# A list scheduler that counts all DMA queues as one resource, and constant matmuls that go on longer, in a sparse attention with two MLPs

## The chip, the cores and the metric

The kernel runs on one core of a Trainium2 chip. The metric is the device time of one launch in microseconds. The five engines are called TensorE (PE, with its weight loads PEld), VectorE (DVE), ScalarE (ACT), GpSimd (POOL) and SyncE (SP). SP only issues transfers; ScalarE and GpSimd issue some too, each on a queue of its own.

## The reference

Four batches, eight heads, 576 positions, head size 64. Four heads see the last 32 positions, four see every 32nd. The result (2304 tokens x 512) goes through two MLPs of width 2048, the first with a squared ReLU and an affine step, the second with a quadratic spline.

```python
def reference(**kw):
    attn_out = _attn_ref(q, k, v)                       # softmax(mask(scale * q k^T)) v
    x = attn_out.transpose(0, 2, 1, 3).reshape(B * S, H * D)
    x = _moe_ref(x, w_in, w_out, s, b)                  # (s * relu(x @ w_in)**2 + b) @ w_out
    return _moe2_ref(x, w_in2, w_out2)                  # h<=-1: 0, h>=1: h, else (h+1)**2/4; then @ w_out2
```

## The kernel before

The weights come as 64-bit words and are decoded on the chip: a piece (128 x 512, 512 KB as 64-bit words) is loaded into one of three `raw` buffers (`decode`, L337), ScalarE makes a float of its upper half (L348), VectorE shifts and joins it (L350, L352). Every operand of an MLP product is split in two (`hi`, `lo`), and each product is three matmuls: hi x hi, hi x lo, lo x hi (`mm3`, L707, and `mm3s`, L949). `weights` (L356) makes the split pieces `w0h`, `w0l` (first matrix) and `w1h`, `w1l` (second matrix) of the first MLP.

The tokens are cut into six units of 384. Attention goes over 21 tiles (`attend`, L439): a strided tile takes some residues of one batch, a local tile 256 tokens. For each tile TensorE writes the mask and the scores (`scores`, L569), VectorE and ScalarE make the softmax (L602 to L627), TensorE transposes it (`flip`, L633), ScalarE or VectorE copies that to SBUF as `pt` (L639), and TensorE forms the values product (`values`, L644), which is split into the MLP's operands `xh` and `xl` (L686 to L692). Half of the first MLP's hidden width is done by plain products (`hidden`, `output`); for the other half the second matrix, and in the second MLP both matrices, use Strassen's scheme with seven products (`product`, `hidden2`, `output2`). For this scheme sums of weight quarters are made on the chip, stored to DRAM through two `pp` buffers by GpSimd's queue (`prepare`, L372, and `parts`, L385; the store is L393), and loaded back by SP when needed (`wmat`, L865).

The order of the work is not written out. Each step is an `Op` with its engines and costs, put into an `Issue` (L109). `order()` (L161) is a list scheduler: backwards from the end it gives each step a due time (with a random offset of 0.3 us from the seed `SEED`), and then, forwards, it always takes the step that can start first, the earlier due time first among equals. Each engine issues its steps in the order of the planned starts; on the chip they wait for semaphores only. The planned times are therefore not those of the chip, but set the order on every engine and queue. MLP products are chained to one another (`pe_op`, L716, and `pe_block`, L946), so that attention products can only be placed between them.

The costs are functions: `dma` (L320) gives a load SP for its bytes at `DMA_RATE`, 390 GB/s, plus 0.08 us for each transfer, and 2.0 us until it has landed. Transfers on ScalarE's queue take 0.45 us of ScalarE each (`load`, L456), the stores (`STORE`, L370) 1.0 us of GpSimd and 4.0 us more to land, and the loads of pieces to prepare get 3.0 us extra (`RAW_LAG`).

While nothing else is ready for TensorE at the start, it multiplies a constant tile: ten times before all (L1180), and in `busy` (L564) before the scores of tiles 1 to 4 and before each tile's transposes, up to three products, if the planned start is before `FILL` = 24 us and as the planned idle time suggests.

Of the kernel before, what the change touches and what calls it, by code (L numbers as in the profile page):

```python
# [13 lines left out]
I64 = mybir.dt.int64  # L14
# [23 lines left out]
SW = 4 * 128 + 2 * RT * NJ + 4 * D  # L38
NEG = -8.0e9
AHEAD = 3.0  # L40
SEED, JITTER = 3, 0.3
WARM = 10
HI_ACT, HOLD, NACC = 12, (0, 1, 3), 6
FILL, MOST = 24.0, 3
RAW, DT, KB, QV, SM, PT, PP, TB = 3, 2, 4, 3, 3, 2, 2, 3
BUFS = {"kb": KB, "qv": QV - 1, "qx": 1, "sm": SM - 1, "sx": 1, "pt": PT}

# [17 lines left out]
G_TAGS = ["w1h", "w1l"] * 4 + ["w1hx", "w1lx"] * 4 + ["kb"] * 4 + ["pi"] * 4 + ["qx", "sx"] + ["qv"] * 2 + ["sm"] * 2 + ["pt"] * 2  # L65
S_TAGS = ["kb"] * 4 + ["qx", "sx"]
SPLIT, SUMMED, SUM_BACK, EVAC2 = (0.0, 6.0, 6.0), (0.0, 0.0, 0.0), 0, 5.0
RAW_LAG, STORE_LAG = 3.0, 4.0
COUNTED = 2
SPACE_A, SPACE_W = 5.2, 2.4  # L70


SUB, MUL, ADD = ALU.subtract, ALU.mult, ALU.add
LATENCY = 0.12
DMA_RATE = 390.0e3
DMA_LATENCY = 2.0
DMA_ISSUE = 0.45
BY_SLOT, ACC_ACT = 3, 0.38


# [28 lines left out]
class Issue:  # L109
# [51 lines left out]
    def order(self):  # L161
# [13 lines left out]
        rng = np.random.default_rng(SEED)  # L175
        for o in self.ops:
            o.due += JITTER * rng.standard_normal() - o.sooner
        free = {"port": 0.0}
        for o in self.ops:
            o.wait, o.ready = len(o.deps), 0.0  # L180
            for x in o.engs:
# [17 lines left out]
        while pool:  # L199
            best = None  # L200
            for o in pool:
                t = room(o)
                if t is None:
                    continue
                for e, d, _, *port in o.engs:
                    at = max(free[e], o.ready, t, free["port"] if port else 0.0)
                    key = (at + (d - min(x[1] for x in o.engs)), o.due, o.n, d, at)
                    if best is None or key < best[0]:
                        best = (key, o, e, d)
            if best is None:  # L210
                raise RuntimeError("the buffers don't suffice")
            (*_, at), o, e, d = best
            _, _, lag, *port = next(x for x in o.engs if x[0] == e)
            pool.remove(o)
            o.start, o.eng, o.idle = at, e, at - free[e]
            free[e] = at + d
            if port:
                free["port"] = at + d
            end = at + d + lag
            for b in o.allocs:  # L220
                b.ring.taken.append(b)
            for b in o.bufs:
                b.left -= 1
                b.end = max(b.end, end + LATENCY)
                b.near = max(b.near, at + d if e == "pe" else end + LATENCY)
            for q in o.succ:
                q.wait -= 1
                q.ready = max(q.ready, at if o in q.behind else at + d if q.engs[0][0] == e == "pe" else end + LATENCY)
                if not q.wait:
                    pool.append(q)  # L230
            done.append(o)
# [11 lines left out]
def sparse_attention_two_mlps(ctx: ExitStack, tc: tile.TileContext, loc, strd, w_ins, w_outs, fixed, out):  # L243
# [27 lines left out]
    op = plan.op  # L271
# [45 lines left out]
    def pool(n):  # L317
        return ("pool", 0.13 + n * 0.00224, 0.1, "port")

    def dma(n, count=1):  # L320
        return ("sp", max(n / DMA_RATE + 0.08 * count, DMA_ISSUE * count), DMA_LATENCY)

    def pe(t):
        return ("pe", t, 0.1)
# [10 lines left out]
    decodes, prepared, pi_line, w_loads, w0_line, w1_line, p_line = [], [], [], [], [], [], []  # L335

    def decode(src, after=(), allocs=(), t=None, line=None, raw=None):  # L337
        late = RAW_LAG if raw else 0.0
        raw = raw or buf(sp, "raw", [128, 2 * DM], I32, RAW)
        t = t or buf(sp, "dt", [128, DM], I32, DT)  # L340
        words = lambda i: raw.tile.rearrange("p (a b) -> p a b", b=2)[:, :, i]
        x = lambda: t.tile.bitcast(F32)
        q_, d_, lag_ = dma(src.shape[0] * src.shape[1] * 8)
        load = op(lambda e: e.dma_start(out=raw.tile.bitcast(I64), in_=src), [(q_, d_, lag_ + late)],
                  writes=[raw], after=after, allocs=allocs, line=line)


        first = op(lambda e: e.activation(out=x(), in_=words(1).bitcast(F32), func=AF.Prelu, scale=2.0 ** -112, alpha=-2.0 ** 32),  # L348
                   [act(DM)], [raw], [t])
        op(lambda e: e.tensor_scalar(out=t.tile, in0=t.tile, scalar1=3, scalar2=None, op0=ALU.logical_shift_left),  # L350
           [dve2(DM, 0.0005)], (), [t])
        op(lambda e: e.scalar_tensor_tensor(out=t.tile, in0=words(0), scalar=29, in1=t.tile,  # L352
                                            op0=ALU.logical_shift_right, op1=ALU.bitwise_or), [dve2(DM)], [raw], [t])
        return t, x, first, load
# [12 lines left out]
        decodes.append(first)  # L367
        wt[g, o] = (hi, lo)

    STORE = lambda nq: ("pool", 1.0, STORE_LAG)  # L370

    def prepare(o, i, early=False):  # L372

# [65 lines left out]
    def attend(i, early):  # L439
# [14 lines left out]
            return buf(wp if tag[0] == "w" else sp, tag, [128, 512], F32, BUFS.get(tag, MS // 2))  # L454

        def load(y, parts, size, queue="sp", line=a_line):  # L456
            ways = [dma(size, len(parts)) if queue == "sp" else ("act", DMA_ISSUE * len(parts), DMA_LATENCY + 2 * size / DMA_RATE)]
            first = bool(w_loads) and not held and line is a_line
            o = op(lambda e, i=i: [e.dma_start(out=f(), in_=x) for f, x in parts], ways, part=[y], line=line,
                   after=[w_loads[k] for k in HOLD] if first else ())  # L460
# [102 lines left out]

        def busy(e, first, out):  # L564

            for _ in range(min(int(first.idle / 0.25 + 0.6), MOST) if first.start < FILL else 0):
                e.matmul(out=out, lhsT=warm_t[:, 0:out.shape[0]], rhs=warm_t[:, 0:out.shape[1]], start=True, stop=True)

        def scores(e, i=i):  # L569
# [72 lines left out]
        pv = [buf(ps, "side", [128, 2, nv], F32, 2) for _ in range(2)]  # L642

        def values(e, i=i):  # L644
            if strided:
                for hp, g in ((hp, g) for g in range(2) for hp in range(2)):
                    for j, _, n, _, _, at_ in (x for x in groups2 if x[1] == g):
# [12 lines left out]
                                e.matmul(out=pv[blk].tile[half(par), hp, c:c + 32], lhsT=v4(pos)[half(blk), s, 2 * hp + par, :],  # L660
                                         rhs=pt.tile[half(blk), 2 * par + pos, r:r + 32], start=True, stop=True)

        op(values, [pe(0.62 if strided else 1.07)], [*vals, pt], pv)

        off, end, cs = (b * S, b * S + S, (2, 3)) if strided else (256 * d, 256 * (d + 1), (0, 1))
        for bank in range(2):
# [611 lines left out]
```

## Time and profile before

| | us |
|---|---|
| median of 3 runs | 839.2 (837.93 to 839.42) |
| the profiled execution | 835.43 |
| its span, first to last instruction | 833.6 |
| TensorE busy | 809.8 (97%) |
| VectorE, ScalarE, GpSimd busy | 627.3, 526.5, 92.3 |
| DMA read and written | 264 GB/s over the span |

Busy time says which engine has work, not which one makes others wait; that is in the chain of work that ended last, followed back from the end, and in the waits. The granted clock is a share of 2.4 GHz; it has two levels here, 0.5 and 1. A mean between them is a stretch with both.

### The profile page before, as it was taken

To read this page: it belongs to the slowest core of one execution; us is meant where nothing else is said; L and a number is where in the kernel's file an instruction comes from. 1 tells how busy PE (TensorE), PEld (TensorE's weight loads), DVE (VectorE), ACT (ScalarE), POOL (GpSimd) and SP (SyncE) were. 2 spreads that over 40 slices of the span, in tenths; PEclk is the share of its full clock that TensorE was granted. 3 is DMA by queue.
4 is the path that set the end of the run, shared out by engine and by line. 5 is a ranking of instruction groups with operands and counts; after the bars stand their busy time and mean duration, and the time that the engine had idled before them with its cause. 6 is when DMAs were issued, how large, how long until landed. Compare 5 with 4: busy or idle time off the path is not lost.

```text
span 833.6 us, 17675 instructions
## 1 busy us (share of the span) xinstructions
PE 809.8 (97%) x6263; PEld 788.5 (95%) x6263; DVE 627.3 (75%) x1335; ACT 526.5 (63%) x1120; POOL 92.3 (11%) x186
## 2 busy tenths in 40 slices
PE   6799999989999999999999999999999999999998
PEld 4679999979899999999998999999999999999998
DVE  4698539879665856768789989997477988466966
ACT  5586545564556666758576677965487854667653
POOL 2110012322212112121111010000000000000000
PEclk9599999999999999999999999999999999999999
DMA  8977484798666759889889899978988889888882
GB/s 260 275 222 253 136 261 159 263 307 276 240 228 246 243 200 335 291 301 337 287 291 314 264 396 386 312 249 270 305 251 256 253 252 293 287 248 253 251 268 94
DMA packets 107261, 221.15 MB, mean 265 GB/s; under 512 B 14118, under 2 KB 29606, under 8 KB 107174
## 3 DMA queue, kind: packets, MB, share of 16 engines
q1 hardware_dynamic: 95906, 182.89, 68.2%
q0 software_dynamic: 10240, 36.71, 11.6%
q8 instruction: 50, 0.82, 0.4%
q10 hardware_dynamic: 1028, 0.43, 0.2%
q14 instruction: 37, 0.30, 0.1%
HBM read 172.27 MB, written 47.71 MB: 264 GB/s over the span
## 4 chain that ended last, share of the span: by engine, by line
PE 89%; DMA 6%; DVE 2%; issue 1%; ACT 1%; SPq 0%; POOL 0%; ACTq 0%; POOLq 0%
PE acc L954 8%; PE acc L953 8%; PE acc L952 8%; PE h L709 8%; PE h L710 7%; PE h L711 7%; PE side L952 6%; PE side L953 6%; PE side L954 6%; PE acc L709 4%; PE h L954 3%; PE h L953 3%; PE h L952 3%; PE acc L710 3%; PE acc L711 3%; DMA kb<-in_strd 2%
## 5 line engine op out<-in xcount | busy, mean ns | idle before, releaser
L393 POOL DMA_DIRECT2D dw<-pp x80 | 55.1, 690 | 273.2 <-DVE pp L391 198.6
L709 PE MATMUL h<-xh,w0h 128*128 128x384 f32 x192 | 66.0, 344 | 0.0
L711 PE MATMUL h<-xh,w0l 128*128 128x384 f32 x192 | 64.8, 337 | 0.7 <-DVE w0l L364 0.7
L709 PE MATMUL h<-xh,w0hx 128*128 128x384 f32 x192 | 65.1, 339 | 0.0
L710 PE MATMUL h<-xl,w0h 128*128 128x384 f32 x192 | 64.8, 338 | 0.0
L711 PE MATMUL h<-xh,w0lx 128*128 128x384 f32 x192 | 64.4, 335 | 0.0
L710 PE MATMUL h<-xl,w0hx 128*128 128x384 f32 x192 | 64.4, 335 | 0.0
L736 ACT ACTIVATE t<-h 128x384 f32<-128x384 f32 x51 | 24.8, 487 | 45.5 <-PE h L711 45.2
L711 PEld LDWEIGHTS h<-xh,w0l 128*128 128x128 f32 x192 | 36.3, 189 | 1.0 <-DVE w0l L364 1.0
L709 PEld LDWEIGHTS h<-xh,w0h 128*128 128x128 f32 x192 | 36.4, 190 | 0.5
L710 PEld LDWEIGHTS h<-xl,w0h 128*128 128x128 f32 x192 | 36.3, 189 | 0.3 <-DVE xl L692 0.3
L709 PEld LDWEIGHTS h<-xh,w0hx 128*128 128x128 f32 x192 | 36.0, 188 | 0.3
L710 PEld LDWEIGHTS h<-xl,w0hx 128*128 128x128 f32 x192 | 36.1, 188 | 0.0
L711 PEld LDWEIGHTS h<-xh,w0lx 128*128 128x128 f32 x192 | 36.0, 188 | 0.0
L328 ACT ACTIVATE gh<-w1h 128x384 fp32r<-128x384 f32 x48 | 24.6, 522 | 14.6 <-PE acc L954 6.3
L999 DVE TENSOR_TENSOR gl<-w1h,gh 128x384 fp32r<-128x384 f32 x48 | 26.4, 555 | 9.6 <-ACT gh L328 9.4
L348 ACT ACTIVATE dt<-raw 128x512 f32<-128x512 f32 x42 | 27.7, 667 | 9.2 <-DMA raw<-in_w_ins 6.8
L709 PE MATMUL acc<-gh,w1hx 128*128 128x384 f32 (+1 forms) x96 | 33.4, 348 | 0.0
L709 PE MATMUL acc<-gh,w1h 128*128 128x384 f32 (+1 forms) x96 | 33.2, 346 | 0.0
L711 PE MATMUL acc<-gh,w1lx 128*128 128x384 f32 (+1 forms) x96 | 32.4, 338 | 0.0
L710 PE MATMUL acc<-gl,w1hx 128*128 128x384 f32 (+1 forms) x96 | 32.4, 338 | 0.0
L711 PE MATMUL acc<-gh,w1l 128*128 128x384 f32 (+1 forms) x96 | 32.4, 337 | 0.0
(581 smaller groups left out, 2790.5 us busy)
## 6 DMA issues: line engine op xcount, KB each, us to landing
dw<-pp POOLq DMA_DIRECT2D x60, 512.0 KB, 4.9
w0h<-dw SPq DMA_DIRECT2D x84, 256.0 KB
w0l<-dw SPq DMA_DIRECT2D x84, 256.0 KB
w0hx<-dw SPq DMA_DIRECT2D x84, 256.0 KB
w0lx<-dw SPq DMA_DIRECT2D x84, 256.0 KB
raw<-in_w_ins SPq DMA_DIRECT2D x32, 512.0 KB
raw<-in_w_outs SPq DMA_DIRECT2D x32, 512.0 KB
kb<-dw SPq DMA_DIRECT2D x56, 256.0 KB
```

What stands on the lines that cost most here:

```text
L328: e.activation(out=out, in_=in_, func=AF.Copy)
L348: first = op(lambda e: e.activation(out=x(), in_=words(1).bitcast(F32), func=AF.Prelu, scale=2.0 ** -112, alpha=-2.0 ** 32), [act(DM)], [r ...
L393: op(lambda e: e.dma_start(out=dw[o][i][qs].rearrange("q p w n -> p q (w n)"), in_=y.tile[:, 0:nq].bitcast(F32).rearrange("p q w n -> p q ...
L709: e.matmul(out=acc, lhsT=wh, rhs=ah, start=first, stop=False)
L710: e.matmul(out=acc, lhsT=wh, rhs=al, start=False, stop=False)
L711: e.matmul(out=acc, lhsT=wl, rhs=ah, start=False, stop=last)
L736: op(lambda e: e.activation(out=c(t), in_=c(p), func=AF.Relu), [act(n)], [p], [t])
L952: e.matmul(out=dst, lhsT=wh, rhs=ah, start=opens and first, stop=False, skip_group_check=not opens)
L953: e.matmul(out=dst, lhsT=wh, rhs=al, start=False, stop=False, skip_group_check=not opens)
L954: e.matmul(out=dst, lhsT=wl, rhs=ah, start=False, stop=last, skip_group_check=not opens)
L999: op(lambda e, g=g, hi=hi, lo=lo: e.tensor_tensor(out=lo.tile[:, 0:n], in0=g.tile, in1=hi.tile[:, 0:n].bitcast(F32), op=SUB), [dve2(n)], [ ...
```

## The change

The planner gets one more resource, `dma`. Every transfer, of whichever queue, starts its bytes when the resource is free, and holds it for its bytes at 300 GB/s before a planned 32 us and 360 GB/s after that, plus 0.08 us for each transfer; it has landed 2.0 us later. SP is taken as occupied until 1.0 us (`KEEP`) before the transfer's bytes are through. A store costs GpSimd 0.75 us instead of 1.0 and its landing follows from the resource instead of 4.0 us; `RAW_LAG` is gone.

The products on the constant tile go on to a planned start of 37 us, up to five at a time, and from a planned 18 us at least two; there are two more calls before each values product, one into each of its two PSUM tiles. The seed of the offsets is another one.

```diff
-SEED, JITTER = 3, 0.3
+SEED, JITTER = 19, 0.3
-FILL, MOST = 24.0, 3
+FILL, MOST, LEAST = 37.0, 5, (18.0, 2)
-RAW_LAG, STORE_LAG = 3.0, 4.0
+KEEP = 1.0
-DMA_RATE = 390.0e3
+DMA_RATES, FULL_FROM = (300.0e3, 360.0e3), 32.0
+POOL_ISSUE = 0.75
...
-            if port:
+            end = at + d + lag
+            if port == ["port"]:
                 free["port"] = at + d
-            end = at + d + lag
+            elif port:
+                _, n, count = port
+                full = max(at + (0.0 if e == "sp" else d), free["dma"])
+                full += n / DMA_RATES[full > FULL_FROM] + 0.08 * count
+                free["dma"], end = full, max(full, at + d) + lag
+                if e == "sp":
+                    free[e] = max(full - KEEP, at + DMA_ISSUE * count)
...
-    def dma(n, count=1):
-        return ("sp", max(n / DMA_RATE + 0.08 * count, DMA_ISSUE * count), DMA_LATENCY)
+    def dma(n, count=1, queue="sp"):
+        long = n / DMA_RATES[1] + 0.08 * count
+        return (queue, max(long, DMA_ISSUE * count) if queue == "sp" else POOL_ISSUE if queue == "pool" else DMA_ISSUE * count,
+                DMA_LATENCY, "dma", n, count)
...
-    STORE = lambda nq: ("pool", 1.0, STORE_LAG)
+    STORE = lambda nq: dma(nq * 512 * 512, 1, "pool")
...
-            ways = [dma(size, len(parts)) if queue == "sp" else ("act", DMA_ISSUE * len(parts), DMA_LATENCY + 2 * size / DMA_RATE)]
+            ways = [dma(size, len(parts), queue)]
...
-            for _ in range(min(int(first.idle / 0.25 + 0.6), MOST) if first.start < FILL else 0):
+            n = max(min(int(first.idle / 0.25 + 0.6), MOST), LEAST[1] * (first.start > LEAST[0]))
+            for _ in range(n if first.start < FILL else 0):
                 e.matmul(out=out, lhsT=warm_t[:, 0:out.shape[0]], rhs=warm_t[:, 0:out.shape[1]], start=True, stop=True)
...
         def values(e, i=i):
+            busy(e, weigh, pv[0].tile.rearrange("p a b -> p (a b)"))
+            busy(e, weigh, pv[1].tile.rearrange("p a b -> p (a b)"))
...
-        op(values, [pe(0.62 if strided else 1.07)], [*vals, pt], pv)
+        weigh = op(values, [pe(0.62 if strided else 1.07)], [*vals, pt], pv)
```

## Rows read from the trace of the kernel before

**Rows 1.** The page: engines' busy time; TensorE's granted clock in 40 slices.
```profile
PE 809.8 (97%) x6263; PEld 788.5 (95%) x6263; DVE 627.3 (75%) x1335; ACT 526.5 (63%) x1120; POOL 92.3 (11%) x186
PEclk9599999999999999999999999999999999999999
```
**Rows 2.** The page: the chain that ended last, shares of the span.
```profile
PE 89%; DMA 6%; DVE 2%; issue 1%; ACT 1%; SPq 0%; POOL 0%; ACTq 0%; POOLq 0%
```
**Rows 3.** Busy time by stretch of the span, with granted clock and DMA.
```profile
core 0: us, PE busy (x) PEld busy (x) DVE busy (x) ACT busy (x) POOL busy (x), PEclk, DMA share, GB/s
...
20.00:25.00 5.00, 3.33 (x96) 2.56 (x96) 3.96 (x13) 2.52 (x10) 1.90 (x3) 0.96 1.04 342
25.00:30.00 5.00, 2.48 (x71) 1.58 (x68) 2.85 (x11) 1.21 (x4) 1.27 (x2) 0.50 0.97 282
30.00:35.00 5.00, 4.20 (x110) 3.73 (x111) 2.73 (x7) 2.85 (x7) 0.23 (x1) 0.50 0.69 234
35.00:40.00 5.00, 4.25 (x103) 3.72 (x99) 4.21 (x10) 2.80 (x9) 1.33 (x4) 0.50 1.03 257
40.00:45.00 5.00, 5.00 (x54) 4.58 (x54) 3.69 (x10) 3.53 (x10) 0.85 (x3) 0.84 0.76 207
...
50.00:60.00 10.00, 8.20 (x125) 6.80 (x124) 10.00 (x24) 8.43 (x22) 1.48 (x3) 1.00 0.63 204
```
**Rows 4.** TensorE's timeline: start us, us, instruction, in brackets idle before and releaser.
```profile
13.64 0.82 PE L567 MATMUL h<-warm_t 128*128 128x512 bf16 x3
...
17.94 0.49 PE L567 MATMUL acc<-warm_t 128*128 128x256 bf16 x3
...
27.46 1.11 PE L636 MATMUL h<-fix_t,sm 128*128 128x128 f32 x4
30.06 1.14 PE L660 MATMUL side<-pt,w1lx 64*64 64x32 f32 x31 [1.48 <-ACT pt L328]
...
37.70 1.14 PE L660 MATMUL side<-pt,qx 64*64 64x32 f32 x31 [0.75 <-ACT pt L328]
...
39.66 0.69 PE L709 MATMUL h<-xh,w0h 128*128 128x384 f32 x1
```
**Rows 5.** The chain in order of time, start: start us, us, what.
```profile
18.96 9.87 DMA raw<-in_w_ins
28.85 0.67 ACT dt L348
...
30.06 2.03 PE side L660 x63
32.09 1.06 PE h L636 x4
...
97.58 1.06 PE side L660 x64
...
102.53 0.44 PE h L636 x4
```
**Rows 6.** The same chain, its four longest DMA pieces after 100 us.
```profile
161.81 6.95 DMA kb<-in_strd
...
171.51 5.95 DMA kb<-in_strd
...
205.70 8.38 DMA dw<-pp
...
443.55 7.48 DMA kb<-dw
```
**Rows 7.** Waits of TensorE: for whom, us in total, times, longest us.
```profile
PE side L580 <- DMA kb<-in_strd: 3.2, 2, 2.6
...
PE h L636 <- DVE sx L627: 2.1, 2, 1.5
PE side L952 <- ACT gh L328: 1.3, 1, 1.3
```
**Rows 8.** The stores of prepared weights, from issue to landing.
```profile
DMA to landing us min/median/max: 2.3/4.9/8.9
```

More of the change, by code (lines that the diff above doesn't have):

```diff
@@ L177, in order @@
             o.due += JITTER * rng.standard_normal() - o.sooner
-        free = {"port": 0.0}
+        free = {"port": 0.0, "dma": 0.0}
         for o in self.ops:
@@ L205, in order @@
                 for e, d, _, *port in o.engs:
-                    at = max(free[e], o.ready, t, free["port"] if port else 0.0)
+                    at = max(free[e], o.ready, t, free["port"] if port == ["port"] else 0.0)
                     key = (at + (d - min(x[1] for x in o.engs)), o.due, o.n, d, at)
@@ L337, in decode @@
     def decode(src, after=(), allocs=(), t=None, line=None, raw=None):
-        late = RAW_LAG if raw else 0.0
         raw = raw or buf(sp, "raw", [128, 2 * DM], I32, RAW)
@@ L342, in decode @@
         x = lambda: t.tile.bitcast(F32)
-        q_, d_, lag_ = dma(src.shape[0] * src.shape[1] * 8)
-        load = op(lambda e: e.dma_start(out=raw.tile.bitcast(I64), in_=src), [(q_, d_, lag_ + late)],
+        load = op(lambda e: e.dma_start(out=raw.tile.bitcast(I64), in_=src), [dma(src.shape[0] * src.shape[1] * 8)],
                   writes=[raw], after=after, allocs=allocs, line=line)
```

## The prediction

> **What bounds the kernel now.** I read the page first: TensorE is busy 97% of the span, and the chain that ended last is TensorE for 89%, DMA for 6% [rows 1, 2]. The reader should see there that no other engine is close (VectorE 75%) and that whatever is to be gained lies in the few places where TensorE stands still, or runs slowly: 833.6 - 809.8 = 23.8 us of idle time, and the stretch of slice 2 where the granted clock is 0.5 of full speed.
>
> Then the table of stretches shows where that is [rows 3]. From 20 to 40 us TensorE is idle for 1.67 + 2.52 + 0.80 + 0.75 = 5.7 us, and from 25 to 40 us it has the lower of its two clocks (granted 0.50, 1.2 GHz instead of 2.4). The timeline of TensorE says what it did around that: after the products on the constant tile at 17.94 there are no more of these, the engine goes from one wait to the next (1.48 us at 30.06, another 0.75 at 37.70), and after the last of these waits it works without a pause into the MLP; in the stretch 40 to 45 the mean clock is back at 0.84, in 50 to 60 at 1.00 [rows 3, 4]. The first MLP product starts at 39.66 [rows 4].
>
> In the chain of the start, the last loads and the softmax of the attention tiles come first, then ScalarE's first weight piece at 28.85, which waited for a load that took 9.87 us, then three times TensorE's values product and two times its transposes in turn [rows 5]. All of these are TensorE's at the low clock. From 40 us on the share of TensorE in the chain hardly breaks: there are three more places, two loads of keys that took 6.95 and 5.95 us, a store that took 8.38 us, and a load of weights that took 7.48 us [rows 6]. TensorE's waits there are 3.2 us in two pieces, up to 2.1 us behind VectorE, and 1.3 us behind ScalarE [rows 7].
>
> The MLP products are chained to each other in the code, so the planner cannot change their order; what the change can move is the place of the attention products among them, the order on the other engines and the queues, and the first 40 us.
>
> **The change part by part.** All sums are against the profiled execution: span 833.6 us, 835.43 us with what lies around it. The median of the three timed runs is 839.2, 3.8 us above it; I take the same difference off the median.
>
> *More products on the constant tile.* They now go on up to a planned 37 us instead of 24, also before the values products (twice each), up to 5 and at least 2 for each call later than 18 us. What they are to buy is the clock. What the low clock costs on the chain: a values product took 2.03 us, later in the same kernel 1.06, so 3 x 0.97 = 2.9 us; the transposes took 1.06 against 0.44, so 2 x 0.62 = 1.2 us [rows 5]; the first six MLP products run from 39.66 to the change of clock about 41.5, some 2 us, and at half the time 1 us [rows 3, 4]. Together 5.1 us, the upper bound of this part; the lower is zero, if the clock falls all the same. I do not take 5.1, since what comes late next is VectorE: it prepares the split weights, has 5 x 4 - (2.85 + 2.73 + 4.21 + 3.69) = 6.5 us idle from 25 to 45, but is busy 10.00 of 10.00 us from 50 to 60, where TensorE is busy only 8.20 [rows 3]. An MLP that begins 4 us earlier meets that engine earlier. I take 3.0 us, some 60%.
>
> *What these products cost themselves.* Three of 256 columns took 0.49 us, three of 512 columns 0.82 [rows 4], so 0.16 and 0.27 each. From the planned 18 us to the MLP I count four transposes and four values products (those that the timeline shows after 21 us). At least 2 per call make 4 x 2 x 0.27 + 4 x 4 x 0.16 = 4.7 us, the most 5 per call make 11.8. The cover is TensorE's idle time, 5.7 us, and the 5.1 that the higher clock would free [rows 3, 5]: the least number fits, the most overruns by about 1 us. Where a transpose is ready and must wait for two of these, it loses up to 0.5 us. Bounds 0 and 2 us lost, I take 0.5, since the count per call follows the planned idle time.
>
> *Transfers of all queues as one resource.* So far a load took its bytes at 390 GB/s on SP's queue alone, ScalarE's and GpSimd's transfers took nothing from it; now all stand in one line at 300, later 360 GB/s, and SP is planned to issue at most 1 us ahead of the data. At the start this moves a step on ScalarE: the decode of the first weight piece stands ahead of the copy that the values product at 30.06 needs, and waits until 28.85 for its load; the transposes that feed the copy began at 27.46 and took 1.11 us, so the copy could have started at 28.6, some 0.9 us before the 29.5 that 28.85 + 0.67 makes [rows 4, 5]. A planner that expects the load later puts the copy first: between 0 and -0.9 us, and beyond it the same VectorE limit; I take -0.5.
>
> In the middle, the two loads of keys that TensorE waited for took 6.95 and 5.95 us from issue [rows 6]; the old planner gives 256 KB about 0.7 + 2.0 us. With stores and weight pieces in the same line a load is planned later, and the scores product that needs it is put behind more MLP products. At best all 3.2 us of waiting go, at worst none, and the new order may make a wait of its own as long as the longest of before, 2.6 us [rows 7]. I take half, -1.6: the plan counts the right cause, yet even the new line with one store ahead (1.5 + 0.8 + 2.0 = 4.3 us) stays below what was measured. Of the wait behind VectorE (1.5 us of 2.1 after a store that took 8.38) and the one in front of the output products (1.3, after a weight load of 7.48) I take 0.4 in all, as the weights' order is fixed [rows 6, 7]. Bounds for all three: -6 and +2.6.
>
> A rule speaks against counting it so. The trace shows a store that landed after 8.38 us where the median is 4.9 and the shortest 2.3 [rows 6, 8], so stores are stretched by what runs beside them. The Trainium skill, page "DMA: Bandwidth & Descriptors", section on queues, rings and completion order, says that each DMA engine goes round its queues packet by packet, so a store is not a block in front of a load, as the new planner has it: both slow each other. By that rule the wait after the store stays and the sum is 0.2 us smaller.
>
> *Removed lags, new seed.* The extra 3.0 us for prepared pieces and the store's 1.0 + 4.0 us are gone; a lone 512 KB store is now 0.75 + 1.54 + 2.0 = 4.3 us, earlier than before. The trace has landings from 2.3 to 8.9 with median 4.9 [rows 8]; I cost it at nothing, because ScalarE is busy 63% [rows 1] and three buffers stand between it and TensorE; the price without that cover is in the last rival. The seed draws new offsets of 0.3 us for every due time: no sign, and I leave it to the range.
>
> Sum: -3.0 + 0.5 - 0.5 - 1.6 - 0.4 = -5.0 us. 835.4 - 5.0 = 830.4 for a profiled execution, 839.2 - 5.0 = **834.2** for the median.
>
> **The rivals.**
> 1. *VectorE takes the gain back.* The MLP starts 4 us earlier but waits for split weights around 50 to 60 us, where TensorE already lost 1.8 us and VectorE has no gap [rows 3]. Then half of the start's gain goes and little comes in the middle: -1.5 - 0.5 - 0.5 = -2.5, so 836.7. For it speaks the full VectorE, against it its 6.5 idle us just before.
> 2. *The clock falls all the same.* The waits inside a scores product (for its second load) and before the sixth tile have no constant products even after the change; if these pull the clock down, the products only run at the low clock too. They cost 0.5 to 1, the ScalarE step and the middle give 1.5: about -0.8, 838.4. Then the change doesn't do what it says. For it speaks that the clock fell while TensorE was busy 3.33 of 5 us [rows 3].
> 3. *Slower: the stores are planned too early.* There are two buffers for stores. A third piece waits on ScalarE, in its in-order queue, until the first has landed; behind it stand the copies that TensorE's next MLP products need. Planned 0.7 us earlier than before, and with pieces decoded up to 3 us earlier in the plan, such a wait grows. In the old order one such store ended in a wait of TensorE of 1.5 us [rows 6, 7]. From the third such wait on (3 x 1.5 = 4.5) it takes more than the 3.0 that the start gives net; four of them, with no gain in the middle, are +6.0 - 3.0 = +3.0, so 842.2. Against it: the shared line also delays stores in the plan where traffic is dense. The skill's rule above would push this way, since it stretches just the stores.
>
> **How the numbers follow.** Forecast 0.50, rival 1 0.20, rival 2 0.14, rival 3 0.16. A measurement of this kernel can tell 0.2% (1.7 us) from no change. The forecast and rival 1 are faster by more than that, rival 2 is within it, rival 3 is slower; a few hundredths of rival 1 spill into "within": faster 0.68, within 0.16, slower 0.16. Range: all bounds at their better end make -5.1 - 0.9 - 6.0 = -12, which I hold for too much at once; the start at its end with the middle at twice its forecast make -5.1 - 0.9 - 4.0 = -10.0, so 829.2, and 828.5 with the 0.7 by which half the spread of the three runs (837.93 to 839.42) can shift it. The high end takes in rivals 1 and 2 and the better half of rival 3: 840.5.
>
> **What would show it.** Right: the granted clock stays 1.00 from 13 us on, values products before the MLP take about 1.06 us instead of 2.03, and the first MLP product starts near 36 us instead of 39.66; ScalarE's copy for the fourth tile's values stands ahead of the first decode; the two waits for keys between 160 and 180 us shrink to under 1.6 us. Wrong: a stretch at 0.50 remains between 25 and 40; or TensorE is idle for more than 2 us between 40 and 60 behind VectorE's split weights (rival 1); or new waits behind ScalarE after store landings appear between 120 and 520 us (rival 3). The prediction fails as a whole if the new order makes waits of many microseconds where TensorE now has none.

## The result and the profile after

| | before | after |
|---|---|---|
| median | 838.93 (22 runs, 835.25 to 843.22) | 843.69 (22 runs, 838.78 to 848.49) |
| ratio, 95% interval | | 1.0051 [1.0035, 1.0068] |
| the profiled execution, its span | 835.43, 833.6 | 843.28, 840.7 |

The change makes the kernel slower by 0.5%, some 4.3 us. The page of after, engines, granted clock and the chain that ended last:

```profile
PE 817.7 (97%) x6308; PEld 793.1 (94%) x6312; DVE 628.7 (75%) x1333; ACT 528.3 (63%) x1122; POOL 91.5 (11%) x186
...
PEclk9999999999999999999999999999999999999999
...
PE 78%; DMA 7%; issue 7%; DVE 5%; POOL 1%; ACT 1%; SPq 1%; ACTq 0%; POOLq 0%; DVEq 0%
```

Against [rows 1, 2]: slice 2 now shows 9 (0.9 or more) in place of 5, so most of the clock came back, and yet the kernel is slower. TensorE's share of the chain fell from 89% to 78%, but that is no measure of the loss: of the 7% "issue", 57 us, some 37 lie in pieces of 1 to 12 us between 367 and 417 us, where the chain runs over GpSimd and its stores while TensorE is busy for 49.79 of 50 us. The chain takes that way because of the stop at 428 us, below.

Where the time went is read with a marker. The two MLPs make 4080 matmuls of 128x384 on TensorE, in the same order in every kernel, so the start of the k-th, from TensorE's timeline, can be set against that of another kernel. The table has the kernel before with the new constant products alone (run e11 below, in the order of before; profiled execution 835.99, median 835.96) and, less that, after (843.28, median 843.69); both executions are typical of their kernels. Below it stand, also less e11, one more execution of e11's order (e13, another seed) and three more of the order of after: e12 and e14 (other seeds), and e1 (with the old constant products). Positive is later.

```
k              0     48     60    108    380    440    560    800   1760   1820   4079
e11, us     41.3   53.1   60.1   69.7  124.0  144.3  194.7  242.7  422.9  433.4  830.4
after      -0.25  +6.52  +3.67  +4.55  +4.55  +6.29  +0.52  +2.27  +3.07  +6.89  +6.55
e13        +0.79  +0.80  +0.95  +0.90  +0.92  +0.93  +0.19  +0.98  +0.98  +0.98  +0.28
e12        -0.09  +5.41  +3.24  +4.15  +4.15  +6.20  +0.34  +2.09  +2.27  +5.00  +4.31
e14        -0.72  +4.76  +1.76  +2.38  +2.38  +4.33  -0.95  +0.76  +3.18  +5.45  +6.60
e1         +0.89  +8.45  +6.60  +7.51  +7.51  +8.70  +2.48  +4.22  +4.26  +4.31  +6.09
```

Four terms for after: +4.6 us up to 70 us, -2.3 from there to 243, +0.8 to 423, +3.8 between 423 and 433, nothing after that (-0.3). The spans differ by 840.7 - 834.2 = 6.5. The places are the same in e12 and e14, the sizes are not: +4.1 and +2.4, -2.1 and -1.6, +0.2 and +2.4, +2.7 and +2.3. In e1 the term at 423 us is +0.1. So a size read from one pair of executions is good to a us or two.

**The start, +4.6.** Stretches of 5 us from 45 to 70 us, TensorE's busy time first, its clock third from the end; after, then e11:

```profile
45.00:50.00 5.00, 4.40 (x55) 3.91 (x54) 3.88 (x9) 3.80 (x10) 2.79 (x6) 1.00 0.85 235
50.00:55.00 5.00, 4.76 (x80) 3.92 (x78) 4.39 (x10) 3.22 (x8) 2.67 (x3) 1.00 0.85 283
55.00:60.00 5.00, 2.29 (x37) 1.86 (x38) 5.00 (x13) 2.19 (x6) 0.30 (x2) 0.80 0.55 200
60.00:65.00 5.00, 5.00 (x55) 4.69 (x55) 4.05 (x12) 3.67 (x13) 0.54 (x1) 0.86 0.55 168
65.00:70.00 5.00, 4.22 (x43) 3.48 (x42) 4.97 (x15) 3.09 (x9) 0.00 (x0) 1.00 0.90 288
```
```profile
45.00:50.00 5.00, 5.00 (x59) 4.58 (x59) 4.67 (x12) 4.08 (x11) 0.23 (x1) 1.00 0.83 233
50.00:55.00 5.00, 4.34 (x47) 3.68 (x46) 5.00 (x11) 4.05 (x8) 1.24 (x2) 1.00 0.71 251
55.00:60.00 5.00, 3.84 (x79) 3.08 (x78) 5.00 (x14) 4.37 (x13) 0.23 (x1) 1.00 0.45 128
60.00:65.00 5.00, 4.95 (x49) 4.32 (x48) 5.00 (x16) 3.66 (x12) 0.00 (x0) 1.00 1.01 329
65.00:70.00 5.00, 5.00 (x30) 5.00 (x29) 3.55 (x8) 3.84 (x8) 0.00 (x0) 1.00 1.06 364
```

TensorE is idle for 25 - 20.67 = 4.3 us in after and for 25 - 23.13 = 1.9 in e11, and in after the clock falls besides (0.80, 0.86). In e14 TensorE has the same wait of 2.9 us, the clock stays at 1.00, and the term is +2.4 instead of +4.6. TensorE's and VectorE's timelines of after say why (line, tile, in brackets idle before and releaser):

```profile
54.22 0.55 PE L589 MATMUL side<-k,q 64*36 64x36 f32 x24
57.71 0.91 PE L645 MATMUL h<-fix_t,sm 128*128 128x128 f32 x4 [2.95 <-DVE sm L636]
58.55 1.12 PE L661 MATMUL side<-pt,qv 54*64 54x54 f32 x32
59.59 0.69 PE L720 MATMUL h<-xh,w0h 128*128 128x384 f32 x1
```
```profile
46.28 0.69 DVE L360 SCALAR_TENSOR_TENSOR dt<-raw,dt 128x512 int32<-128x512 int32 x1
...
52.31 0.94 DVE L636 TENSOR_TENSOR sm<-sm,dn 128x512 f32<-128x512 f32 x1
...
56.41 0.64 DVE L360 SCALAR_TENSOR_TENSOR dt<-raw,dt 128x512 int32<-128x512 int32 x1
56.97 0.68 DVE L636 TENSOR_TENSOR sm<-sm,dn 128x512 f32<-128x512 f32 x1
57.57 0.75 DVE L628 TENSOR_TENSOR sx<-side,mx 128x256 f32<-128x256 f32 x2
58.24 0.68 DVE L372 TENSOR_TENSOR w0l<-dt,w0h 128x512 fp32r<-128x512 f32 x1
```

and VectorE in e11, where the same instructions are L352, L628 and L364:

```profile
50.96 0.68 DVE L352 SCALAR_TENSOR_TENSOR dt<-raw,dt 128x512 int32<-128x512 int32 x1
...
52.93 1.26 DVE L364 TENSOR_TENSOR w0l<-dt,w0h 128x512 fp32r<-128x512 f32 x1
54.12 0.68 DVE L628 TENSOR_TENSOR sm<-sm,dn 128x512 f32<-128x512 f32 x1
```

The fifth weight piece is joined on VectorE at 56.41 instead of 50.96, because the new order puts the softmax of two tiles ahead of it. The MLP products that need it (k=48) come at 59.59 instead of 53.1; TensorE has nothing left in front of them but the transposes and the values product of the next tile, and stands 2.95 us behind VectorE: by its releaser, for that tile's softmax (`sm`, 56.97), which VectorE takes right after the join.

**The middle, -2.3.** The two waits for keys of [rows 7] are gone: between 150 and 185 us no wait of TensorE is left in after. Of 4.0 us gained by 195 us (+4.55 to +0.52), 1.8 are given back by 243.

**The stop at 428 us, +3.8.** ScalarE's timeline, then TensorE's, then the stretches:

```profile
422.06 0.93 ACT L338 ACTIVATE gh<-g_xl 128x384 fp32r<-128x384 f32 x2
427.79 0.63 ACT L338 ACTIVATE pp<-sm 128x512 fp32r<-128x512 f32 x1 [4.81 <-DMA dw<-pp]
428.33 0.47 ACT L747 ACTIVATE w1hx<-h 128x384 f32<-128x384 f32 x1
```
```profile
428.85 0.44 PE L720 MATMUL h<-xh,w0hx 128*128 128x384 f32 x1 [2.00 <-ACT w1hx L747]
```
```profile
425.00:430.00 5.00, 3.00 (x17) 2.67 (x16) 1.54 (x4) 1.95 (x4) 0.00 (x0) 1.00 0.96 377
430.00:435.00 5.00, 5.00 (x22) 5.00 (x21) 4.24 (x12) 4.81 (x10) 1.28 (x2) 0.66 0.46 172
```

ScalarE stands for 4.81 us in front of a copy into a store's buffer that is not free until an earlier store has landed. Behind it in its queue is the evacuation that frees TensorE's accumulator. TensorE waits 2.00 us and then has a mean granted clock of 0.66 for a stretch; together they cost 3.8 in this execution. The lower clock does not always follow. In e12 and e14 the same stop is 2.47 and 2.04 us long, and the stretch behind it (e12 first) has the full clock, so it cost 2.7 and 2.3:

```profile
430.00:435.00 5.00, 5.00 (x31) 5.00 (x30) 4.68 (x12) 4.93 (x11) 1.28 (x2) 1.00 0.56 193
```
```profile
430.00:435.00 5.00, 5.00 (x30) 5.00 (x29) 4.27 (x11) 4.69 (x10) 1.28 (x2) 1.00 0.52 173
```

And in e1, where VectorE and ScalarE have the same order, ScalarE waits too, but TensorE does not: the store landed after 5.10 us, against 6.06, 6.95 and 5.73 in after, e12 and e14, and TensorE was itself 1.2 us later than in after (k=1760):

```profile
425.42 0.63 ACT L338 ACTIVATE pp<-sm 128x512 fp32r<-128x512 f32 x1 [3.71 <-DMA dw<-pp]
```

### The profile page after: what moved, and what is told of

Same layout as the page of the kernel before. It is cut to its first block, busy times and chain, and to the rows that moved or that the text cites. A ratio compares the mean times of both kernels' runs of the same rounds, so it can differ in the third digit from the quotient of the medians.

```text
span 840.7 us, 17752 instructions
## 1 busy us (share of the span) xinstructions
PE 817.7 (97%) x6308; PEld 793.1 (94%) x6312; DVE 628.7 (75%) x1333; ACT 528.3 (63%) x1122; POOL 91.5 (11%) x186
## 4 chain that ended last, share of the span: by engine, by line
PE 78%; DMA 7%; issue 7%; DVE 5%; POOL 1%; ACT 1%; SPq 1%; ACTq 0%; POOLq 0%; DVEq 0%
PE acc L963 7%; PE acc L964 7%; PE acc L965 7%; PE h L720 6%; PE side L964 6%; PE side L963 6%; PE side L965 6%; PE h L721 6%; PE h L722 5%; PE h L964 3%; PE h L963 3%; PE h L965 3%; PE acc L720 3%; DMA dw<-pp 3%; PE acc L721 3%
## 5 line engine op out<-in xcount | busy, mean ns | idle before, releaser
L356 ACT ACTIVATE dt<-raw 128x512 f32<-128x512 f32 x42 | 27.7, 668 | 12.5 <-DMA raw<-in_w_outs 4.7
L338 ACT ACTIVATE gh<-w1h 128x384 fp32r<-128x384 f32 x48 | 24.6, 523 | 14.4 <-PE acc L965 6.3
L399 DVE TENSOR_TENSOR pp<-dt,pp 128x512 fp32r<-128x512 f32 (+1 forms) x36 | 22.3, 619 | 14.0 <-ACT pp L338 13.9
```

The source lines that it names most:

```text
L338: e.activation(out=out, in_=in_, func=AF.Copy)
L399: op(lambda e: e.tensor_tensor(out=y.tile[:, 0:nq, 1, :], in0=x(), in1=y.tile[:, 0:nq, 0, :].bitcast(F32), op=SUB), [dve2(256 * nq)], [b], ...
```

## The experiments

Theories at the outset: A, the first planned rate (300 GB/s) puts the decode late, the raw buffers stay full and SP's loads stand behind them; C, the new seed redraws the order; and the new products or the late model as the cost. Each time is a median of 6 to 12 runs beside 22 to 34 of before on the same chip; there were three chips, so between groups of runs the ratios are the better measure.

**Parts undone, seed 19.** e1: the old constant products in the changed kernel.

```diff
-FILL, MOST, LEAST = 37.0, 5, (18.0, 2)
+FILL, MOST = 24.0, 3
```


> The changed kernel with the products on the constant tile as before (planned start up to 24 us, up to three, none before the values products); the order of everything else is that of the changed kernel. Theory A (the first 45 us are planned with loads later than they come, so VectorE and ScalarE take tile 0's last softmax steps before tile 1's first and decode the first weight piece late, which holds SP's queue): the order is what costs, so the 108th MLP product still comes 5 us later than in the kernel before, or more if the granted clock falls to 0.50 again around 25 to 40 us: 843 to 846 us. Theory B (the added products themselves cost it: TensorE's work of some 5 us and a pause of 1.9 us at 31.4 us): that loss goes, 839 to 840 us.

842.39, ratio 1.0034 [1.0015, 1.0053], beside 843.69 of after (1.0051): within the intervals no difference, so no gain from the products shows in the new order. They do keep the clock up: the mean granted clock of the 12 runs of e1 is 0.981, of the 22 of after 0.990.

e3: the seed put back.

```diff
-SEED, JITTER = 19, 0.3
+SEED, JITTER = 3, 0.3
```


> The changed kernel with the seed of the kernel before (3). Theory A: the planner's rates set the order at the start, so tile 1's first maximum still stands behind tile 0's normalisation and the MLP lags by 3 to 5 us at 100 us: 841 to 844 us; waits in the middle are others. Theory C (the new seed drew a bad order): the lag at 100 us is under 1 us, 836 to 839 us.

842.82, 1.0029 [1.0009, 1.005]. The seed isn't what makes the changed kernel slow.

e5 and e6: the old transfer model for transfers planned before 45 us (this diff), and for those from 45 us on.

```diff
...
+                if at < 45.0:
+                    free[e] = at + (1.0 if e == "pool" else max(n / 390e3 + 0.08 * count, DMA_ISSUE * count) if e == "sp" else d)
+                    end = free[e] + (4.0 if e == "pool" else lag + late if e == "sp" else lag + 2 * n / 390e3)
+                    free["dma"] = max(free["dma"], end - 2.0)
...
```


> The changed kernel, but transfers that the plan issues before 45 us are planned as before (each queue on its own, 390 GB/s on SP); later ones as in the change; seed 19 and the new products on the constant tile stay. Theory A: the lag of 5.35 us at the 108th MLP product goes to between -3 and +1, first MLP product at 36 to 39 us, in all 835 to 839 us. Theory B or C: the lag stays at 4 to 6 us, 843 to 845 us.

> The changed kernel, but transfers that the plan issues after 45 us are planned as before (own queues, 390 GB/s, landing of stores 5.0 us after their issue, prepared pieces 3.0 us later). Theory A: the lag at the 108th MLP product stays at about 5.3 us; the two waits for keys between 160 and 180 us come back (+3), the wait of TensorE behind ScalarE and a store at about 428 us (2.0 us of waiting and 1.7 us of low clock) goes: 842 to 844 us. If the late part of the plan were the cause instead, 838 to 839 us.

846.93, 1.008 [1.0053, 1.0107], and 844.43, 1.0042 [1.0015, 1.0069]. Undoing either half doesn't bring the time back; e5 is slower than any of the theories had it. In e6 a wait for keys of 2.6 us is back, so the late model is what removed it; in e5 the start became worse (+8.6 against before at k=108).

**Parts alone, on the kernel before.** e2: the new constant products. e4: the new seed.

```diff
-SEED, JITTER = 3, 0.3
+SEED, JITTER = 19, 0.3
```


> The kernel before with only the second half of the change: the products on the constant tile go on to a planned 37 us, up to five, at least two after 18 us, also before the values products. The order of all else is that of the kernel before. If the clock was worth what the prediction took (3.0 us less 0.5): 836 to 837 us, first MLP product at 36 to 37 us, granted clock 1.00 from 25 to 40. If VectorE or SP's queue sets the start (rival 1): the clock stays up and the time does not move, 838.5 to 840 us, the lag at the 108th MLP product between -1 and +1.

> The kernel before with seed 19 instead of 3, nothing else. If the seed is no cause: 837 to 841 us and a lag at the 108th MLP product within 1.5 us of before. If seed 19 draws a bad order in itself (as the changed kernel's wait behind a store at 428 us, which stayed with the old late costs, might say): 842 to 845 us.

e2: 837.22, 0.9978 [0.9952, 1.0004]. The time is near what was expected if the clock is worth 2.5 us, but the first MLP product comes at 44.63, not at 36 to 37. e4: 845.52, 1.0071 [1.0048, 1.0093]: the seed alone costs 6 us in the old planner. Its stretches show another place than after's:

```profile
60.00:65.00 5.00, 3.42 (x93) 2.33 (x84) 4.97 (x12) 2.23 (x8) 0.68 (x1) 1.00 0.69 234
65.00:70.00 5.00, 1.21 (x24) 0.95 (x24) 4.71 (x11) 3.15 (x6) 0.00 (x0) 0.82 0.99 365
70.00:75.00 5.00, 3.04 (x8) 2.64 (x9) 4.14 (x12) 3.20 (x9) 0.23 (x1) 0.50 0.66 193
```

TensorE is idle for 7.3 us there, and works at the lower clock from 70 us on.

**Theory A by itself.** e7: 390 GB/s as the first rate. e10: the first weight piece planned to land 6 us earlier.

```diff
-DMA_RATES, FULL_FROM = (300.0e3, 360.0e3), 32.0
+DMA_RATES, FULL_FROM = (390.0e3, 360.0e3), 32.0
```
```diff
+        if not w_loads:
+            way = (*way[:2], way[2] - 6.0, *way[3:])
```


> The changed kernel with 390 instead of 300 GB/s up to the planned 32 us; all else as in the change. In the order, tile 1's maximum stands before tile 0's normalisation again, and the first weight piece is decoded on VectorE ahead of the fourth tile's low parts. If the early rate is the cause of the lag: SP's fourth load of a weight piece at 31 to 33 us instead of 36.6, lag at the 108th MLP product -1 to +1.5 us, 838.5 to 841 us. If sharing and the 1 us limit on SP are the cause whatever the rate: lag 2 to 5 us, 842 to 844 us.

> The changed kernel, but the first weight piece's load alone is planned to land 6.0 us earlier; that moves its decode on VectorE from behind the fourth tile's low parts to before the third's. If the late decode (a raw buffer that is held, SP's queue blocked behind it, DMA idle from 31 to 38 us) is the larger part of the lag: SP's fourth load of a piece at 30 to 32 us, lag at the 108th MLP product 0 to +1.5 us, 839 to 841 us. If the earlier delay (tile 1's maximum behind tile 0's normalisation, 3.15 us of idle VectorE) is the larger part: lag 2 to 4 us, 841.5 to 843.5 us.

847.39, 1.0096 [1.0063, 1.013], and 846.05, 1.0079 [1.0051, 1.0106]. Both did what they were to do (SP's fourth weight load at 31.2 and 31.7 us instead of 36.6) and both are slower than either reading allowed. A, as stated, fell: an early fourth load is not what is missing.

**Pairs of seeds.** Now D (the order of before is a good draw, the models hardly differ) against E (the new model itself costs). e11 and e13 are e2 with SEED 7 and 11, e12 and e14 are after with them.

> The kernel before with the new products on the constant tile, and SEED 7 in place of 3; the old transfer model. With the seeds 3 and 19 the old model has given 837.2 (with these products) and 845.5 (without them), so the draw alone moved it by some 6 to 8 us. Theory D (the order of the kernel before is a good draw, the models hardly differ): 841 to 847, as the seven other orders run so far. Theory E (the new model itself costs 3 to 5 us against the old one at the same seed): 835 to 839 here and 840 to 844 for the new model with seed 7.

> The changed kernel with SEED 7 in place of 19: the new transfer model and the new products, the pair of the run above. Theory D: 841 to 847, within 4 us of its pair on either side. Theory E: 3 to 5 us slower than its pair.

> The kernel before with the new products on the constant tile, and SEED 11; the old transfer model. Theory D: 841 to 847. Theory E: 835 to 839.

> The changed kernel with SEED 11: the new transfer model and the new products, the pair of the run above. Theory D: 841 to 847, on either side of its pair. Theory E: 3 to 5 us slower than its pair.

| | SEED 3 | 7 | 11 | 19 |
|---|---|---|---|---|
| old model, new products | 837.22 (e2) | 835.96 | 837.27 | 845.52 (e4, old products) |
| ratio | 0.9978 | 0.9960 [0.9937, 0.9984] | 0.9971 [0.9943, 0.9999] | 1.0071 |
| new model, new products | 842.82 (e3) | 844.95 | 842.63 | 843.69 (after) |
| ratio | 1.0029 | 1.0053 [1.0031, 1.0076] | 1.0029 [1.0005, 1.0053] | 1.0051 |

E was right for three seeds, and D fell: with seeds 3, 7 and 11 the new model is 5.4 to 9.0 us slower than the old one (seed 3 on two chips, 4.3 us by the ratios). With seed 19 it is not: there the old model is the slower by its ratio, though with the old products. And the table holds fewer draws than it seems. The order of the instructions on VectorE and ScalarE, read from the programs, is the same to 99% or more in every tenth of the program for seeds 3, 7 and 11 of the old model, and again for 7, 11 and 19 of the new one. An offset of 0.3 us rarely turns a decision, and where it does (19 in the old model, 3 in the new) all that follows is another order. So the six runs measure two programs, three times each: the mean ratio of the first is 0.9970, of the second 1.0044, and their distance, 0.74% or 6.2 us, is close to the 6.5 us of the marker table.

**The form of the start.** What differs is where VectorE's joins of the weights stand in its order. In the old model with seeds 3, 7 and 11 the first five are its 56th, 64th, 71st, 76th and 92nd instruction (first form); in the new one with 7, 11 and 19 its 60th, 71st, 73rd, 80th and 100th (second); in the old one with 19 its 58th, 68th, 69th, 81st and 90th (third), with three weight loads in a row on SP. Theory F: the form decides. e15 and e18 are e5 with seeds 3 and 7, which give the first and the third form; e16 is e7 with seed 3 (first form; in its trace each join stands one place later); e17 is e11 with 300 GB/s:

```diff
-DMA_RATE = 390.0e3
+DMA_RATE = 300.0e3
```


> The changed kernel with the old transfer model for everything planned before 45 us, the new one from there on, the new products on the constant tile, and SEED 3. In its program the first five joins of the decode are the 56th, 64th, 71st, 76th and 92nd of VectorE's instructions, as in the kernel before and as with seeds 7 and 11 there (the first form of the start; the changed kernel has 60, 71, 73, 80, 100 with four seeds, the second form). Theory F (the form of the start decides, and the late model is worth the 2.6 us of the waits for keys): 833.5 to 836, faster than both kernels. Theory E2 (the late model itself costs, by the stop at 428 us): 838 to 841.

> The changed kernel with 390 in place of 300 GB/s as the first planned rate, and SEED 3; one line for all queues, KEEP and the late model stay. Its first joins stand at 56, 64, 71, 76, 92 on VectorE, the first form of the start. Theory F: 834 to 838, against 842.8 with 300 GB/s and the same seed. If the single line itself or KEEP costs, whatever the rate: 841 to 844.

> The kernel before with the new products on the constant tile, SEED 7, and DMA_RATE 300 in place of 390 GB/s in the old model; all else is the run at 836.0. Its first joins stand at 61, 71, 73, 81, 98 on VectorE, close to the second form. Theory F with the planned rate as the cause of the form: 840 to 845. If the rate is harmless outside the single line: 835 to 838.

> As the first run of these four (old model before 45 us, new one after it), with SEED 7. Here the joins stand at 57, 67, 68, 80, 94 on VectorE and SP's fifth to seventh weight piece are 26th to 28th of its loads instead of 27th, 31st and 32nd: a third form, that of the kernel before with seed 19 (845.5), of the changed kernel with the old early model and seed 19 (846.9) and of 390 GB/s with seed 19 (847.4). Theory F: 843 to 847, although the seed and the early model are those of the run at 836.0. If seed and early model decide and not the form: 834 to 836.

838.85, 1.0003 [0.9981, 1.0026]; 840.1, 1.0008 [0.9984, 1.0032]; 859.9, 1.0233 [1.0195, 1.0271]; 844.76, 1.0058 [1.0033, 1.0084]. e18 is F's plainest hit: seed and early model of the good runs, but the third form, and a time from the middle of 843 to 847. e16 is 2.7 us below e3, the same kernel with 300 GB/s (on another chip, and the intervals overlap). e15 and e16 came out 2 to 3 us above what F wanted, e15 in the range of E2 (the late model itself costs), and e17 far beyond: by the marker it is 12.5 us behind e11 at k=108, and loses 9.4 us more near 565 us, where TensorE waits 6.75 us for ScalarE's `gh`. TensorE's idle time from 45 to 75 us, 30 less the busy time of its six stretches, in all profiled executions:

```
first form    before 1.8  e2 2.4  e11 1.9  e13 2.0  e15 3.0  e16 1.0  (e19 1.9  e20 1.0, below)
second form   after 4.3  e12 3.7  e14 3.9  e1 3.7  e3 3.7  e6 3.7  e10 3.7
third form    e4 7.3  e5 5.8  e7 5.9  e18 5.4        e17 5.4
```

The three forms don't overlap, and it is the form, neither the seed nor the half of the model, that sorts them (e3, whose joins are two places earlier than the second form's, is counted there). Counted from the first MLP product to k=108, which leaves out what came before, they are 27.7 to 29.8, 31.5 to 35.0 and 37.7 to 40.4 us. The medians follow in the main: 836.0 to 840.1, 842.4 to 846.1, 844.8 to 847.4; the last two overlap. The exception is e17 (41.0 us to k=108), close to the second form by its joins, but not by its time. So the form sorts the start; the whole time also hangs on stops behind it. What is late in the second form was shown above, and it is in all executions of that program; this is TensorE's longest wait between 44 and 72 us in e12, and in e14, and then the longest in e11:

```profile
PE h L645 <- DVE sm L636: 2.9, 1, 2.9
```
```profile
PE h L645 <- DVE sm L636: 2.9, 1, 2.9
```
```profile
PE h L714 <- DVE w0l L364: 0.7, 1, 0.7
```

Why e15 and e16 weren't faster still: both gained the middle (e16 is at -2.6 us against e11 from 243 to 433 us), and lost it at 447 and 546 us. ScalarE's timeline and TensorE's in e16 at the first of these, and the clock behind it:

```profile
448.42 0.63 ACT L338 ACTIVATE pp<-qv 128x512 fp32r<-128x512 f32 x1 [3.43 <-DMA dw<-pp]
...
450.06 0.51 ACT L338 ACTIVATE pt<-w1h 128x384 fp32r<-128x384 f32 x1
```
```profile
450.62 0.69 PE L963 MATMUL acc<-pt,sx 128*128 128x384 f32 x1 [3.19 <-ACT pt L338]
```
```profile
450.00:455.00 5.00, 4.38 (x13) 4.07 (x14) 4.27 (x9) 4.57 (x10) 0.00 (x0) 0.50 0.66 218
```

That is the stop of after at 428 us once more: a store's landing, ScalarE's queue, TensorE, the clock; +4.0 us by the marker. At 546 us TensorE waits 1.5 us for ScalarE's `gh` and 1.2 for VectorE's `gl`, +4.4.

**The late model in the middle only.** e19 is e15 with the old model after a planned 300 us, e20 is e16 with it.

```diff
-                if at < 45.0:
+                if at < 45.0 or at > 300.0:
```


> The new products on the constant tile, SEED 3, the old transfer model for transfers planned before 45 us and after 300 us, the new model only between. In its program VectorE's and ScalarE's last half stand in the order of the kernel before. Theory F: the start of the first form stays, the 3.3 us gained between 145 and 220 us stay, and the stops at 447 and 546 us (4 us each with the clock's fall behind them) go: 831 to 835. If the stops hang on what was planned before 300 us: 838 to 841, as with the new model to the end (838.85).

> The new products on the constant tile, SEED 3, the new transfer model with 390 GB/s as the first rate up to 300 us, the old model from there on. Theory F: the profiled execution with 390 GB/s and the new model to the end was 2.6 us ahead of the best order of the old model (836.0) until 433 us, and lost 4.0 and 4.4 us at 447 and 546; without these stops 832 to 835. If the stops hang on what was planned before 300 us: 838 to 841.

838.38, 0.9973 [0.9939, 1.0008], and 835.96, 0.9962 [0.9936, 0.9989]. e19 missed what F wanted and lies where the stops were to stay; e20 missed by 1 us. With these two, F's times came true in one run of six. The stop at 546 us is gone in both, so that one belongs to the order that the late model makes with seed 3 (after, e12 and e14 don't have it). The other isn't the late model's alone: e19 and e6 have it too, with the old model there (ScalarE idle for 4.47 us up to 427.20, and for 3.82 up to 425.73, for a store's landing; TensorE behind it for 2.15 and 2.10), and e20 has 0.4. Which plan makes a copy wait for a store's landing isn't settled; one execution of each is all there is. e20 is faster than both kernels of the change, and no faster than the kernel before with the new products alone (0.9960 to 0.9978).

## Why the prediction was wrong

**The bound and the clock: right in the main.** TensorE and its few stops are what counts. The granted clock is 1.00 from 20 to 30 us, and then:

```profile
30.00:35.00 5.00, 2.49 (x70) 1.89 (x72) 3.04 (x10) 0.73 (x3) 0.07 (x1) 0.91 0.22 81
35.00:40.00 5.00, 4.84 (x83) 3.52 (x82) 3.52 (x11) 2.59 (x8) 0.00 (x0) 0.75 0.48 165
```

It is 0.50 from 34.1 to 37.5, after a pause of 1.92 us (below), where before had 0.50 from 24.6 to 41.6. So the sign "1.00 from 13 us on" failed for 3.4 us.

**The constant products, -3.0 + 0.5: right in size on the old order, by luck in part; worth nothing that shows in the new one.** On the order of before three runs give 0.9978, 0.9960 and 0.9971, by their mean -2.5 us, and the mean granted clock of their runs is 0.994 to 0.995, where the 140 later runs of before have some 0.982. But the way there, "the first MLP product near 36 us", was wrong: it comes at 41.07 in after and at 44.63, 41.32 and 42.11 in the three runs, later than the 39.66 of before. No trace shows where the 2.5 us were won. Between the transposes at 34.99 and 40.66 TensorE makes 14 constant products, 10 of which took 2.07 us, and the last transposes before the MLP wait for VectorE. In the changed kernel the start then runs into VectorE at 55 us, as rival 1 had it, and e1 shows no gain from the products. Rival 1 had the place and the engine, though it took the cause to be an earlier MLP and capped the loss at half of the gain.

**The ScalarE step, -0.5: happened, and gave nothing.** The copy stands at 27.29, ahead of the decode at 29.39. The values product that it feeds stood behind another tile's scores until 30.87, then met a pause of 1.92 us (below), and the MLP waits for VectorE after that.

**Transfers as one line, at the start: the step that failed.** I asked what a later expected load does to ScalarE's order alone and took it for a gain of up to 0.9 us. The same later load moves every decode on VectorE's queue too, and there, from 50 to 60 us, [rows 3] already showed an engine without a gap. Putting the fifth join behind two softmaxes cost 4.6 us in after, 4.1 and 2.4 in e12 and e14. "No sign, and I leave it to the range" for the seed was the same omission: the range gave 0.7 us to the spread of the runs and nothing to another order, where another order of the same work costs 6 us and more (e4, e7, e17).

**The waits for keys, -1.6: right.** Both are gone, and the middle gave 2.3 us net (2.1 and 1.6 in e12 and e14). It took the late model (e6 has the wait again). For the two other waits, -0.4, the runs show no gain that can be told: after has 0.81 us behind VectorE, at 134.85 (1.5 in before), and 1.77 for a load in front of the output products, at 458.69 (1.3 in before).

**Stores, costed at nothing: the other step that failed.** The mechanism is rival 3's, word for word: a piece in ScalarE's in-order queue behind a landing. The term that the sum put at nothing measured 3.8, 2.7 and 2.3 us in after, e12 and e14, and 0.1 in e1. I also priced such a wait by its length alone (1.5 us); in after the lower clock came behind it, and 2.0 us of waiting measured 3.8. The store in question was issued at 421.65 and took 6.06 us to land, where the plan has 4.3. The Trainium skill, page "DMA: Bandwidth & Descriptors", section on queues, rings and completion order, says that each DMA engine goes round its queues packet by packet. The 6.06 us are in line with that, but no run shows what stretched this store, nor did one test the rule.

Together, against before: -2.5 (products) + 4.6 - 2.3 + 0.8 + 3.8 - 0.3 = +4.1, where the ratio gives +4.3. That it fits so well is luck: with e12 in the place of after the sum is +1.8, with e14 +4.1.

Two things about the base. The execution of before that I read (835.43) was 3.5 us below its median; its mean granted clock, 0.988, is reached by 4 of the 140 later runs of before, so it had less of the low clock to win back than most. And the shown cause ends at the order: no run moved the fifth join alone; that the planned rate of 300 GB/s draws the second form is well supported (the new model gave it, or a close one, with four seeds, and 390 GB/s with seed 3 gave the first), but 390 GB/s with seed 19 gave the third, so a better rate is no cure.

## What to carry to other kernels

A list scheduler's cost model is judged by the order that it produces, on every engine's queue: before believing in a truer cost, list what moved on the engine that has no gap, and ask what then stands behind it. Compare models over several orders, and look whether two seeds give two programs at all; here six runs were two. Price a wait of TensorE as a range, from its own length to that with the lower clock behind it, and trace more than one execution: one order gave 0.1 to 3.8 us at the same place.

## What the runs showed of the hardware

TensorE stands still for up to 4.0 us around 31 us, with no other engine and no load of data that it waits for by the trace ("issue"). It differs from execution to execution, also of one program: 1.92 in after, 1.9 in e12 and 0.7 in e14; 2.7 in e2, 1.4 in e11, none over 0.3 in e13; 4.0 in e1; 0.2 in before; none in e4 and e17. This is the line of after:

```profile
33.32 0.37 PE L671 MATMUL side<-pt,w1lx 64*64 64x32 f32 x11 [1.92 <-issue]
```

The traces on hand say what it waits for. Their DMA records have transfers of 16 KB of the kind "instruction" on queue 8: in after 51 of them, and TensorE's trace has 13044 instructions, so one for each 256. One such transfer ends shortly before each of these pauses does:

```
us                            after    e12    e14    e11     e2     e1
the 16 KB transfer ends       31.98  32.08  32.99  30.86  32.86  30.31
TensorE goes on               33.32  33.44  34.34  32.32  34.46  31.67
```

The same holds for all 26 pauses over 0.4 us that the 20 traces put down to "issue" after the first 5 us: each ends 1.2 to 1.6 us after such a transfer. And in after, e12 and e14 the pause stands in front of the same instruction. So TensorE most likely stood without its next instructions; no run was made to test it, and why the transfer came late is open. That the engines wait for semaphores only, as said of the kernel before, is then not all. The pause may be part of the spread of the times (9.7 us between the fastest and the slowest of the 22 runs of after), and one profile prices a start no better than that.

The clock fell after a stop of 2.00 us in after (mean 0.66 in the stretch behind) and of 3.19 us in e16 (0.50). It stayed at 1.00 after stops of 2.47 us in e12, 2.04 in e14 and 2.10 in e6 at the same place, after the 2.9 us wait of e14 near 55 us, and after the 0.7 us waits of e11 between 45 and 75 us. So one such stop can cost the clock or not.
